# A Mamba-2 scan and its hardswish MLP on one core: the opening stage reordered

## The chip, the core and the metric

The kernel runs on one core of one Trainium2 chip. The core has five engines with an instruction list each: TensorE (PE in the profile; its weight loads are the row PEld), VectorE (DVE), ScalarE (ACT), GpSimd (POOL) and SyncE (SP, which here only issues transfers). They run beside each other and wait for one another by semaphores. Sixteen transfer engines (DMA) move data between the chip's memory and the core's. The metric is device microseconds of the one core, lower is better.

## The reference

The input `x` has 4 batches, 8 heads, 768 tokens and 32 channels; `B` and `C` have 16 states per head, `a` one decay per token. Per batch and head the scan is

```
cum   = cumsum(log(clip(a, 1e-6, 1)))                 # within a chunk
y     = ((C B^T) * exp(cum_i - cum_j) * (i >= j)) x   # within the chunk
      + (C state) * exp(cum_i)                        # from before it
state = exp(sum log a) * state + sum_j B_j x_j exp(cum_end - cum_j)
```

and its output, 3072 tokens of 256 channels, goes through an MLP: `h = y w_in` (256 to 2048), `g = h * clip(h + 3, 0, 6) / 6`, `out = g w_out` (2048 to 256). The MLP weights are 64-bit floats in memory.

## The kernel before

Tokens are worked in six chunks of 128 (times four batches: 512 columns). The order of every engine's list is written out by hand. Chunk 0 has a stage of its own: its scan, then its MLP in plain float32 products (`mlp_in` at L681, `first_out` at L801) while the weights are still being decoded. Chunks 1 to 5 use products of split operands (`squares`, `cross`, `wide_units`, `last_out`). The change touches the stage of chunk 0 and the first part of chunk 1's.

**Opening, to the first MLP product.** `a` comes in on SP's queue, then `C` (`pairs_first`, L99, eight transfers of 32 KB), `x` (L118) and weight piece 1 (`load_w`, L130). ACT's queue issues weight piece 0 and `B`. While `a` travels, PE writes the causal masks of chunks 0 and 1 into eight banks (`diff_mask`, L348), with thirty one-column products in between as filler. DVE scans the logs, `cum` (L288), and splits it into three bf16 parts, `split` (`in_three`, L293, last operation at L300). PE then adds to each bank the differences cum_i - cum_j: `diff_less` (L375) the subtrahend, `diff_pick` (L381) the minuend. For the first two batches of chunk 0 the minuend takes sixteen narrow products, one per head and half; for the other six (chunk, batch) pairs it takes two wide ones from rows that DVE first spreads over the heads (`spread_rows`, L277 to L281). ACT takes the exponentials (`diff_exp`, L400): four banks of chunk 0, later two of chunk 1, whose banks the state needs. `first_eto` (L402) and `turn_b` (L462) follow on PE and ACT. DVE transposes `C` (`turn_squares`, L500), masks it by parity (`part_heads`, L510) and applies `fade` (L516); PE multiplies the identity as filler (`busy`, L525). `scores` (L551) are 64 record pairs at L565 followed by the state's at L583; ACT copies the state (`take`, L599), DVE multiplies the scores with the decays (`multiply`, L614), PE forms the output in two halves (`mix`, L660, and `from_state`, L538), ACT copies it out (`keep`, L676), and `mlp_in` begins.

**Weights.** Each of eight pieces (four of `w_in`, four of `w_out`, 1 MB each as raw 64-bit words) is decoded to float32 by `decode` (L190): ACT copies the top 16 bits (L202), DVE takes the significand (L207, L211) and masks exponent and sign (L221, L223), ACT moves the exponent in two activations (L227, L229), DVE joins (L234) and multiplies (L244). It is a generator, and `weights(i, n)` advances it by n steps. There are three raw buffers; `load_w` for piece i + 3 waits for piece i to be read. A one-element `memset` into a buffer holds a transfer until DVE gets to it (L143, for piece 2 alone).

**First MLP.** `mlp_in(0, f)` for f = 0 to 15 uses four banks in turn, so f waits for the DVE operation at L798 (`times_ramp`) of f - 4, and every fourth f for the next piece of `w_in`. DVE decodes the pieces in between (`weave`, L1179). After it `first_out` runs in four passes of four batches; between them stand, among others, four PE transposes of `cum` (`turn_cum`, L334) with DVE's `by_token` (L338), which give the decays per token for chunks 2 to 5 (`cum_n`, first used by ACT at L420), the new state (`renew`, L631), the stores and loads of the decay rows on SP (`store_rows`, `load_eto`, `rows`), and the splitting of `w_in` (`in_parts`, L702).

## Time and profile before

| what | value |
|---|---|
| median of 3 runs | 337.93 us (337.47 to 337.95) |
| the profiled execution's own time | 337.99 us |
| its span | 336.2 us |
| PE busy | 329.7 us, 98% of the span |
| DVE busy | 265.4 us, 79% |
| ACT busy | 207.8 us, 62% |
| first MLP product of chunk 0 (L686) begins | 21.44 us |
| `first_out` of chunk 0 (L811) begins | 49.19 us |

Times inside an execution are microseconds from the span's start. The profile gives busy time per engine, the chain of work that ended last (each step followed back to what released it), groups of instructions by source line with what ended the idle time before them, and stretches of time with each engine's busy share. Matmuls are pipelined and their ends are modelled, so the distance from start to start is the better measure on PE. A float32 product shows as two records. "issue" is time in which an engine waited for nothing that the profile shows.

### The profile page before, as it was taken

The numbers are of one execution on the slowest core, as the hardware profiler recorded it, in microseconds if no ns is written. First come the engines' busy times: TensorE is split into PE (matmuls) and PEld (weight loads), VectorE is DVE, ScalarE is ACT, GpSimd is POOL, SyncE is SP. The second block draws the span as 40 slices with busy tenths as digits, with TensorE's granted clock in tenths as the row PEclk, the third lists the DMA queues.
The fourth block names the chain that finished last, engine by engine and source line by source line (L and its number), as shares of the span: only waits on it lengthen the run. The fifth ranks groups of instructions, "written<-read, shape, count | busy, mean of one in ns | idle before, by whom it ended". The sixth has DMA issues, their size and how long they took to land.

```text
span 336.2 us, 8325 instructions
## 1 busy us (share of the span) xinstructions
PE 329.7 (98%) x3361; PEld 272.4 (81%) x3361; DVE 265.4 (79%) x418; ACT 207.8 (62%) x448; POOL 130.3 (39%) x124
## 2 busy tenths in 40 slices
PE   7999999999999999999999999999999999999995
PEld 5464788888778888888888888888888888899994
DVE  6889999977899729969949558938678958599973
ACT  4788887747987571677662577643487221677661
POOL 2200000180744796179983078771058740000000
PEclk9999999999999999999999999999999999999999
DMA  8969960655950215229207258100142001210001
GB/s 174 168 251 225 197 253 19 171 75 140 178 39 1 61 34 116 47 35 108 49 2 162 36 73 76 37 4 10 27 71 20 2 4 17 29 20 0 2 0 62
DMA packets 89605, 25.15 MB, mean 75 GB/s; under 512 B 82208, under 2 KB 85952, under 8 KB 89056
## 3 DMA queue, kind: packets, MB, share of 16 engines
q1 hardware_dynamic: 85184, 23.33, 37.3%
q10 hardware_dynamic: 4384, 1.31, 1.8%
q8 instruction: 26, 0.43, 0.5%
q14 instruction: 11, 0.09, 0.1%
HBM read 21.33 MB, written 3.29 MB: 73 GB/s over the span
## 4 chain that ended last, share of the span: by engine, by line
PE 98%; POOL 0%; issue 0%; DVE 0%; ACT 0%; POOLq 0%
PE h L754 33%; PE wb L1002 9%; PE wc L1002 8%; PE o L811 8%; PE h L686 8%; PE wa L1002 8%; PE o_end L966 6%; PE wb L1010 3%; PE y L660 3%; PE y L538 2%; PE cb L565 2%; PE d L363 1%; PE y L583 1%; PE d L376 1%; PE d L528 1%; PE o_end L984 1%
## 5 line engine op out<-in xcount | busy, mean ns | idle before, releaser
L798 DVE SCALAR_TENSOR_TENSOR gT<-gT,h 128x512 f32<-128x512 f32 x96 | 64.6, 684 | 21.2 <-ACT gT L793 19.6
L793 ACT ACTIVATE gT<-h,half 128x512 f32<-128x512 f32 x96 | 65.4, 683 | 23.4 <-PE h L754 21.0
L774 ACT ACTIVATE h<-h 128x512 f32<-128x512 f32 x66 | 38.3, 585 | 36.6 <-PE h L754 36.5
L754 PE MATMUL h<-y_hi,w_part 128*128 128x512 f32 x160 | 51.1, 405 | 0.0
L754 PE MATMUL h<-y_less,w_part 128*128 128x512 f32 x160 | 50.1, 399 | 0.0
L754 PE MATMUL h<-y_lo,w_part 128*128 128x512 f32 x160 | 49.5, 395 | 0.0
L857 POOL TENSOR_TENSOR s<-gT 128x512 f32<-128x512 f32 x16 | 25.3, 1579 | 51.4 <-DVE gT L798 51.4
L754 PEld LDWEIGHTS h<-y_hi,w_part 128*128 128x128 f32 x160 | 29.9, 188 | 7.3 <-DVE gT L798 0.9
L754 PEld LDWEIGHTS h<-y_lo,w_part 128*128 128x128 f32 x160 | 30.0, 188 | 6.9
L420 ACT ACTIVATE L<-L,cum_n 128x64 f32<-128x64 f32 x128 | 31.7, 337 | 4.5 <-POOL L L162 4.5
L754 PEld LDWEIGHTS h<-y_less,w_part 128*128 128x128 f32 x160 | 29.1, 188 | 6.1 <-DVE h L771 0.3
L811 PE MATMUL o<-w_out,gT 128*128 128x256 f32 x128 | 29.1, 381 | 0.0
L686 PE MATMUL h<-yT,w_in 128*128 128x256 f32 (+1 forms) x96 | 27.8, 451 | 0.0
L438 POOL TENSOR_TENSOR tmp<-state,eto 128x256 f32<-128x256 f32 x5 | 3.4, 680 | 62.7 <-DVE state L593 56.0
L811 PEld LDWEIGHTS o<-w_out,gT 128*128 128x128 f32 x128 | 24.0, 190 | 3.4
L686 PEld LDWEIGHTS h<-yT,w_in 128*128 128x128 f32 x96 | 18.2, 190 | 9.3 <-issue 6.7
L857 POOL TENSOR_TENSOR gT<-gT 128x512 f32<-128x512 f32 x16 | 23.9, 1498 | 0.7
L894 DVE TENSOR_TENSOR q_part<-gT,q_part 128x256 fp32r<-128x256 f32 x24 | 21.5, 926 | 0.0
L431 POOL TENSOR_TENSOR bs<-B,L 128x128 f32<-128x128 f32 x24 | 12.0, 523 | 23.6 <-ACT L L420 15.7
L966 PE MATMUL o_end<-v_pair,g_pair 128*128 128x256 f32 x120 | 21.1, 281 | 0.0
L162 POOL TENSOR_SCALAR_AFFINE_SELECT L<-L 64x1024 f32<-64x1024 f32 (+1 forms) x16 | 20.0, 1255 | 2.0 <-DMA L<-cum_d 1.5
L857 POOL TENSOR_TENSOR s<-s,gT 128x512 f32<-128x512 f32 x16 | 20.5, 1290 | 0.0
(164 smaller groups left out, 636.0 us busy)
## 6 DMA issues: line engine op xcount, KB each, us to landing
raw<-in_moe_w_out_dram SPq DMA_DIRECT2D x4, 1024.0 KB
L<-cum_d SPq DMA_DIRECT2D x8, 512.0 KB
xt<-in_x_dram SPq DMA_DIRECT2D x6, 512.0 KB
raw<-in_moe_w_in_dram SPq DMA_DIRECT2D x3, 1024.0 KB
out_dram<-back SPq DMA_DIRECT2D x128, 16.0 KB
pairs<-in_C_dram SPq DMA_DIRECT2D x40, 32.0 KB
B<-in_B_dram SPq DMA_DIRECT2D x5, 256.0 KB
eto<-cum_e SPq DMA_DIRECT2D x20, 64.0 KB
```

What stands on the lines that cost most here:

```text
L162: nc.gpsimd.affine_select(out=t[rows], in_=t[rows], pattern=pattern, compare_op=ALU.is_ge, fill=-1e5, base=base, channel_multiplier=-1)
L420: nc.scalar.activation(Ls[c][:, b, h], Ls[c][:, b, h], AF.Exp, bias=cum_n[:, c, g:g + 1])
L686: nc.tensor.matmul(out=h[:, t:t + n], lhsT=w_in[f // FP][:, j, f % FP * P:(f % FP + 1) * P], rhs=yTs[k][:, j].rearrange("p b i -> p (b i)" ...
L754: nc.tensor.matmul(out=hs_[k, f], lhsT=w[j][:, f % FP * P:(f % FP + 1) * P], rhs=y[:, j], start=(start and j == 0), stop=True, skip_group_ ...
L774: nc.scalar.activation(h, h, AF.Copy, scale=1.0 / EPS + 1.0)
L793: nc.scalar.activation(gTs[k][:, f], h, AF.Relu, bias=half, scale=1.0 / 6.0)
L798: nc.vector.scalar_tensor_tensor(out=g, in0=g, scalar=1.0, in1=h, op0=ALU.min, op1=ALU.mult)
L811: nc.tensor.matmul(out=o[:, b % 2], lhsT=gTs[0][:, f, b * P:(b + 1) * P], rhs=w_out[:, f], start=(f == 0 and b % 2 == 0), stop=True, skip_ ...
L857: nc.gpsimd.tensor_tensor(out=o, in0=p_, in1=q_, op=op)
L894: nc.vector.tensor_tensor(out=l[:, j], in0=g[:, j], in1=h[:, j].bitcast(FP32), op=ALU.subtract)
L966: nc.tensor.matmul(out=ends_["cross" if n == 2 else "squares"][b], lhsT=g_parts[t][n][:, b * P:(b + 1) * P], rhs=w, start=(t == 0 and b < ...
L1002: nc.tensor.matmul(out=bank[:, slot], lhsT=lhs[:, j], rhs=rhs[:, j], start=(clear and j == 0), stop=True, skip_group_check=True)
```

## The change

- `C` of chunk 0 is loaded by head instead of by batch and head parity: still eight transfers of 32 KB, but the slowest dimension of each is now 32 groups of tokens rather than 4 heads.
- `x` of chunk 0 and weight piece 1 get a holding `memset`; `x` is issued after the first significand step of piece 0, piece 1 after `fade`.
- All (chunk, batch) pairs form their minuend by the sixteen narrow products; `spread_rows` and its two selectors go, and so do the thirty one-column products and `busy`.
- Piece 1 of the weights is decoded by a function of its own after `keep`, its exponents and results in two halves.
- In the first MLP, where a step of `weights` joins a piece (f = 4, 8, 12), it stands between `ramp` and `times_ramp`; the last sixteen products are no longer cut in two; the second significand step moves up one step.
- `renew(0)` moves from `first_out` to before `mix(0)`.
- `cum` by token comes from four small transfers, a DVE transpose and a POOL operation instead of PE transposes.
- The third piece of `w_in` is split earlier, and the buffers that `w_part` and `y_hi` take over change places.

```diff
@@ -100,2 +100,9 @@
             t = loads.tile([P, 2, NB, 4, N], FP32, name="pairs", tag="bc")
+            if c == 0:
+                for h in range(NH):
+                    rows = slice(h // 2 * 32, h // 2 * 32 + 32)
+                    nc.sync.dma_start(
+                        out=t[rows, h % 2].rearrange("s b a n -> s b (a n)"),
+                        in_=src[:, h, sl, :].rearrange("b (s a) n -> s b (a n)", a=4))
+                return t
             for b in range(NB):
@@ -120,2 +127,4 @@
         xts[c] = loads.tile([P, NB * NH, D], FP32, name="xt", bufs=1)
+        if c == 0:
+            nc.vector.memset(xts[c][:, 0, :1], 0)
         nc.sync.dma_start(out=xts[c], in_=x[:, :, sl, :].rearrange("b h s d -> s (b h) d"))
@@ -141,3 +150,3 @@
         raws[i] = raw
-        if i == 2:
+        if 0 < i < 3:
             nc.vector.memset(raw[:, :1], 0)
@@ -147,4 +156,2 @@
     load_bc(0)
-    load_x(0)
-    load_w(1)
     nc.scalar.preload_act_table_set("natural_log_exp_and_others")
@@ -189,2 +196,36 @@
 
+    def decode_halves(i):
+
+        n, cut = NK * FP * P, FP * P // 2
+        top = raws[i].bitcast(U16).rearrange("p (k f w) -> p k f w", k=NK, w=4)[..., 3]
+        lo, hi = (raws[i].rearrange("p (n w) -> p n w", w=2)[:, :, w] for w in range(2))
+        s = att.tile([P, n], U16, name="ws").rearrange("p (k f) -> p k f", k=NK)
+        e = att.tile([P, n], U16, name="we").rearrange("p (k f) -> p k f", k=NK)
+        m = att.tile([P, n], U32, name="wm")
+        halves = [slice(h * cut, (h + 1) * cut) for h in range(2)]
+        for h in halves:
+            nc.scalar.copy(out=s[:, :, h], in_=top[:, :, h])
+        nc.vector.tensor_scalar(
+            out=m, in0=hi, scalar1=0xFFFFF, scalar2=0x100000,
+            op0=ALU.bitwise_and, op1=ALU.bitwise_or)
+        for h in halves:
+            for t, mask in ((e, 0x7FF0), (s, 0x8000)):
+                nc.vector.tensor_scalar(
+                    out=t[:, :, h], in0=s[:, :, h], scalar1=mask, scalar2=None,
+                    op0=ALU.bitwise_and)
+            nc.scalar.activation(
+                e[:, :, h].bitcast(BF16), e[:, :, h], AF.Relu, bias=bias_hi, scale=-8.0)
+            nc.scalar.activation(
+                e[:, :, h], e[:, :, h].bitcast(BF16), AF.Relu, bias=bias_lo, scale=-1.0)
+        nc.vector.scalar_tensor_tensor(
+            out=m.bitcast(FP32), in0=lo, scalar=2.0 ** -32, in1=m, op0=ALU.mult, op1=ALU.add)
+        load_w(i + NRAW)
+        m = m.bitcast(FP32).rearrange("p (k f) -> p k f", k=NK)
+        for h in halves:
+            nc.vector.tensor_tensor(
+                out=e[:, :, h], in0=e[:, :, h], in1=s[:, :, h], op=ALU.bitwise_or)
+            nc.vector.scalar_tensor_tensor(
+                out=w_in[i][:, :, h], in0=m[:, :, h], scalar=2.0 ** -20,
+                in1=e[:, :, h].bitcast(BF16), op0=ALU.mult, op1=ALU.mult)
+
     def decode(i):
@@ -200,6 +241,3 @@
         m = att.tile([P, n], U32, name="wm")
-        for sl in (slice(0, n),) if i != 1 else (slice(0, n // 2), slice(n // 2, n)):
-            nc.scalar.copy(out=s[:, sl], in_=top[:, sl])
-            if i == 1 and sl.start == 0:
-                yield
+        nc.scalar.copy(out=s, in_=top)
 
@@ -218,2 +256,3 @@
             next(parts_m)
+            load_x(0)
             next(parts_m)
@@ -227,6 +266,6 @@
         nc.scalar.activation(e.bitcast(BF16), e, AF.Relu, bias=bias_hi, scale=-8.0)
+        next(parts_m, None)
         yield
         nc.scalar.activation(e, e.bitcast(BF16), AF.Relu, bias=bias_lo, scale=-1.0)
-        next(parts_m, None)
-        if i and i + NRAW < 2 * NP:
+        if i > 1 and i + NRAW < 2 * NP:
             load_w(i + NRAW)
@@ -254,5 +293,2 @@
     low = pre[:G, 10, :2 * P]
-    spread = [pre[:, 11 + c].bitcast(BF16).rearrange("k (h i) -> k h i", h=NH) for c in range(2)]
-    of_batch = const.tile([P, NB], BF16, name="of_batch")
-    of_head = const.tile([P, NH], BF16, name="of_head")
 
@@ -266,6 +302,2 @@
                 op=ALU.add)
-            nc.vector.tensor_reduce(
-                out=of_batch, in_=pick.rearrange("k (b h) -> k b h", b=NB), axis=AX.X, op=ALU.add)
-            nc.vector.tensor_reduce(
-                out=of_head, in_=pick.rearrange("k (b h) -> k h b", b=NB), axis=AX.X, op=ALU.add)
         nc.scalar.mul(less, pick, -1.0)
@@ -276,8 +308,2 @@
 
-    def spread_rows(c):
-
-        nc.vector.tensor_tensor(
-            out=spread[c], in0=split[:, c].unsqueeze(1).to_broadcast([P, NH, P]),
-            in1=of_head.unsqueeze(2).to_broadcast([P, NH, P]), op=ALU.mult)
-
     def log_a(sl):
@@ -333,9 +359,16 @@
 
-    def turn_cum(c_ps):
-        for c in range(2, NC):
-            nc.tensor.transpose(out=c_ps[:, c], in_=cum_c[:, c], identity=ident[:G, :G])
+    def spread_cum():
 
-    def by_token(c_ps):
-        nc.vector.tensor_scalar(
-            out=cum_n[:, 2:], in0=c_ps[:, 2:], scalar1=-1.0, scalar2=None, op0=ALU.mult)
+        cum_q = ffn.tile([P, NC - 2, G], FP32, name="cum_q", tag="wide")
+        for q in range(4):
+            nc.sync.dma_start(
+                out=cum_q[q * G:(q + 1) * G], in_=cum_c[:, 2:, q * G:(q + 1) * G])
+        return cum_q
+
+    def by_token(cum_q):
+        cum_t = ffn.tile([P, NC - 2, G], FP32, name="cum_t", tag="back")
+        nc.vector.transpose(
+            out=cum_t.rearrange("p c g -> p (c g)"), in_=cum_q.rearrange("p c t -> p (c t)"))
+        nc.gpsimd.tensor_scalar(
+            out=cum_n[:, 2:], in0=cum_t, scalar1=-1.0, scalar2=None, op0=ALU.mult)
 
@@ -355,7 +388,2 @@
             d = ps_y.tile([P, NH, HT], FP32, name="d", tag=f"y{b % 2}")
-        if (c, b) == (0, NB - 1):
-            for _ in range(30):
-                nc.tensor.matmul(
-                    out=d[:1, 0, :1], lhsT=ident_h[:, :1], rhs=hide[:, :1], start=True, stop=True,
-                    skip_group_check=True)
         n = NH // 4
@@ -381,9 +409,2 @@
     def diff_pick(c, b):
-        if c or b >= 2:
-            for a, rows in enumerate(HALF):
-                nc.tensor.matmul(
-                    out=ds[c, b][rows], lhsT=of_batch[:, b:b + 1].to_broadcast([P, HT]),
-                    rhs=spread[c][:, :, rows], start=False, stop=True,
-                    tile_position=(0, a * HT), skip_group_check=True)
-            return
         for h in range(NH):
@@ -524,9 +545,2 @@
 
-    def busy(n, bank):
-
-        for _ in range(n):
-            nc.tensor.matmul(
-                out=bank.rearrange("p (b i) -> p b i", b=NB), lhsT=ident,
-                rhs=ident.unsqueeze(1).to_broadcast([P, NB, P]), start=True, stop=True)
-
     def from_state(c, a, pairs=range(NQ)):
@@ -680,6 +694,6 @@
 
-    def mlp_in(k, f):
+    def mlp_in(k, f, between):
         h = ps.tile([P, TB], FP32, name="h", tag=f"f{f % 4}")
         for j in range(NK):
-            n = TB // (1 + (f * NK + j >= NF * NK - 16))
+            n = TB // (1 + (f * NK + j >= NF * NK - 0))
             for t in range(0, TB, n):
@@ -690,9 +704,5 @@
         ramp(k, f, h)
+        between()
         times_ramp(k, f, h)
 
-
-
-
-
-
     NJ = NF // 2
@@ -718,3 +728,3 @@
 
-        hi = one(const, f"w{i - 1}" if i > 1 else f"hi{i}")
+        hi = one(const, {2: "w0", 3: "w2"}.get(i, f"hi{i}"))
         lo = one(const, f"lo{i}") if i < 2 else one(att, "wm") if i == 2 else two("ws")
@@ -734,3 +744,3 @@
     def split_y(k):
-        hi = const.tile([P, NK, TB], F32R, name="y_hi", tag="w0")
+        hi = const.tile([P, NK, TB], F32R, name="y_hi", tag="w1")
         lo = att.tile([P, NK, TB], F32R, name="y_lo", bufs=1)
@@ -886,3 +896,3 @@
         hi, lo, less = quarter_parts[k] = [], [], []
-        homes = ((ffn, "wide"), (ffn, "back")), ((const, "w0"), (att, "y_lo"))
+        homes = ((ffn, "wide"), (ffn, "back")), ((const, "w1"), (att, "y_lo"))
         for where, g in zip(homes, halves):
@@ -1106,5 +1116,6 @@
 
-    def results(c):
+    def results(c, more=None):
         if c == 1:
             keep(c)
+            next(more)
         split_y(c)
@@ -1142,7 +1153,5 @@
         mask_again(0, b)
-    for c in range(2):
-        spread_rows(c)
+    weights(0, 1)
     diff(0, 0, 1)
     diff(0, 2, 3)
-    weights(0, 1)
     for b in range(NB):
@@ -1150,8 +1159,7 @@
     first_eto()
-    diff(1, 2, 3)
     weights(0, 1)
+    turn_b(0)
+    diff(1, 2, 3)
     for b in range(NB):
         ends(0, b)
-    turn_b(0)
-    diff(1, 0, 1)
     weights(0, 2)
@@ -1159,2 +1167,3 @@
     diff_exp(1, 3)
+    diff(1, 0, 1)
     turn_squares(bcs[0][0], turned(0)[2])
@@ -1162,14 +1171,13 @@
     fade(0, HALF[1])
+    load_w(1)
     weights(0, 1)
-    busy(2, ps.tile([P, NB * P], FP32, name="d", tag="f3"))
     scores(0)
     multiply(0)
+    weights(0, 1)
     load_w(2)
     load_w(3)
-    weights(0, 1)
-    weights(1, 1)
+    renew(0)
     mix(0)
-    keep(0, lambda: weights(1, 1))
-    weights(1, 3)
-    weights(1, 1)
+    keep(0)
+    decode_halves(1)
     load_bc(1)
@@ -1188,5 +1196,7 @@
             for f in range(NF):
-                mlp_in(k, f)
+                late = [i for i in weave.get(f, []) if f == 4 * i - 4]
+                mlp_in(k, f, lambda: [weights(i, 1) for i in late])
                 for i in weave.get(f, []):
-                    weights(i, 1)
+                    if i not in late:
+                        weights(i, 1)
                 if f in (6, 8):
@@ -1195,2 +1205,3 @@
             add_up(ends_at[1])
+            cum_q = spread_cum()
             store_rows()
@@ -1209,8 +1220,4 @@
                         next(ins[n])
-                    if (i, b) == (1, 0):
-                        renew(0)
                     if (i, b) == (1, 1):
-                        c_ps = ps.tile([P, NC, G], FP32, name="c_ps", tag="f1")
-                        turn_cum(c_ps)
-                        by_token(c_ps)
+                        by_token(cum_q)
                     if (i, b) == (2, 0):
@@ -1227,3 +1234,3 @@
                         load_bc(ahead)
-                        for n in (0, 0, 1):
+                        for n in (0, 0, 1, 2):
                             next(ins[n])
@@ -1239,4 +1246,3 @@
                         own_products(c)
-                        results(c)
-                        next(ins[2])
+                        results(c, ins[2])
                         decay(ahead, 2)
@@ -1251,3 +1257,2 @@
             next(ins[2])
-            next(ins[2])
             continue
```

More of the change, by code (lines that the diff above doesn't have):

```diff
@@ L1162 @@
     fade(0, HALF[1])
+    load_w(1)
     weights(0, 1)
-    busy(2, ps.tile([P, NB * P], FP32, name="d", tag="f3"))
     scores(0)
     multiply(0)
+    weights(0, 1)
     load_w(2)
     load_w(3)
-    weights(0, 1)
-    weights(1, 1)
+    renew(0)
     mix(0)
-    keep(0, lambda: weights(1, 1))
-    weights(1, 3)
-    weights(1, 1)
+    keep(0)
+    decode_halves(1)
     load_bc(1)
```

## The prediction

> **What bounds the kernel now.** I read the page first (PE busy 98% of the span, and 98% of the chain that ended last), then the chain in order of time, then ACT, DVE and the transfers of the first 22 us. From 21.44 us on the chain is PE without a break worth 0.1 us, so a saving counts only if it starts PE's first MLP product earlier or takes work from PE's own list. The chain of waits, columns start, length, what:

> ```profile
> 6.63 1.28 PE d L371 x3
> 7.92 0.85 PE d L376 x2
> 8.77 0.99 PE d L392 x17
> 9.76 0.60 PE d L376 x2
> ...
> 17.65 0.38 ACT adds L599
> ...
> 19.62 0.26 PE y L660 x12
> 19.88 0.20 issue
> 20.08 0.75 PE y L660 x44
> 20.83 0.61 PE y L538 x16
> 21.44 27.74 PE h L686 x96
> ...
> 59.55 0.36 PE c_ps L336 x4
> ```

> See three things: two L376 products take 0.85 us at 7.92 but 0.43 from 11.14 on, so PE runs at half rate until about 9.9 us; a wait for ACT's `adds` stands in the middle; and PE waits 0.20 us for nothing but its next instruction. Then ACT and DVE in order of time:

> ```profile
> 9.38 1.08 ACT L400 ACTIVATE L<-d 128x512 f32<-128x512 f32 x2 [1.40 <-PE d L392]
> 10.74 1.08 ACT L400 ACTIVATE L<-d 128x512 f32<-128x512 f32 x2 [0.28 <-PE d L384]
> 12.75 0.59 ACT L466 COPY bT<-t_ps 128x512 f32<-128x512 f32 x1 [0.64 <-PE t_ps L457]
> 15.47 1.06 ACT L400 ACTIVATE L<-d 128x512 f32<-128x512 f32 x2
> 7.42 2.36 DVE L279 TENSOR_TENSOR pre<-split,of_head 128x1024 bf16<-128x1024 bf16 x2
> 13.02 1.12 DVE L500 STREAM_TRANSPOSE csT<-pairs 128x512 f32<-128x512 f32 x1 [0.27 <-DMA pairs<-in_C_dram]
> ```

> ACT goes almost without a gap from 9.38 to 16.53. The last pair of exponentials frees the banks into which L583 adds the state; L583 begins at 16.75 and feeds `adds`, which feeds L660. So ACT's list, not C or DVE, is what ends last before the MLP. The last view is the stretches of the transfers (the last two columns are the share of the 16 transfer engines and GB/s):

> ```profile
> 8.00:9.00 1.00, 1.00 (x14) 0.30 (x14) 1.00 (x2) 0.00 (x0) 0.00 (x0) 1.00 0.40 44
> 18.00:19.00 1.00, 0.93 (x66) 0.84 (x67) 1.00 (x3) 1.00 (x4) 0.00 (x0) 1.00 0.01 4
> ```

> From 8 to 11 us only some 0.4 of the engines work, on C and the tail of B; at 18 us all is loaded.

> **The change part by part.**

> *Spread rows and fillers out, head products in.* DVE loses L279 (2.36 us) and two reductions (0.39 us). PE loses 30 one-column products (0.82 us in the chain), the four L528 (1.91 us), and six pairs of wide picks; it gains 6 x 16 narrow ones. Sixteen narrow ones took half of 0.99, 0.50 us, at half rate, the four wide of two batches 0.55, 0.28 each: +0.22 x 6 = 1.3 us of PE before the scores, less at full rate. Without the fillers L371 ends near 6.9, so the first L376 starts when its weights follow `split` (DVE L300 ends 7.39), at 7.55 instead of 7.71. PE then goes: batch 0, 1 to 9.4; L376 to 10.1; first half of the next batch 10.4; all 10.9; `e_ps` and `t_ps` to 11.8; the four of chunk 1 (2 x 0.43 and 2 x 0.5, with the 0.1 gaps of the trace) to 13.3-13.5. Scores can start then, against 15.54.

> *DVE.* After 7.39: L207 0.73, memset 0.06, L211 1.14, L221 0.45, L223 0.46, L500 1.12, L510 0.88: `cT` at 12.3, if C has landed by 10.3. C now spreads over 16 engines instead of some 0.4 of them, so it and B should be in by about 10; if not, the cost is that of today's landing (12.9), which puts `cT` at 15.0, still before today's 15.1.

> *ACT, the deciding list.* First pair of exponentials 9.22-10.30 (-0.16); third starts when its product has drained, 10.7 (no spread to wait for, and `t_ps` now stands ahead of chunk 1, so the 0.64 wait goes); fourth ends 11.75, `eto` 12.1, `bT` 12.64, L227 and L229 (1.18 and 1.06 start to start) 14.88, chunk 1's pair 15.95 instead of 16.53: 0.58 us. L583 follows at 16.2, `adds` at 17.1, and L660 begins 0.58 earlier, at 17.5. DVE covers this: L234 waits for L229 and ends 15.65, two L614 end 16.9. From L660 to the MLP the trace has 3.3 us, of which the wait at 19.88, with its emptied pipe, is 0.2 to 0.4. MLP start 20.4 to 20.8; I take 20.6, so **-0.77 us**.

> *x and weights held.* x goes out behind DVE's L207 (8.2, not 9.61) and has 4 us of packets, so it lands near 13.5; L583 needs it at 16.2. Piece 1 goes out behind the `fade` (12.8, not 10.31 behind x) and takes some 4.5 us: 17.5, needed when `keep` ends at 21. Cost nothing, with 3 us to spare. Pieces 2 and 3 go out as now (19.2, 19.4).

> *Piece 1 in halves, `renew` forward.* `renew` (0.45 + 0.6 us of DVE) now stands before piece 1's decoding; that is hidden by `keep`. ACT does two copies and four activations of half size after `keep` (bounded by 0.34 us, half of a whole 0.68, and 0.68 each; near the upper end, as a 512-wide copy took 0.68 with its latency): first half of w_in[1] at 24.9, second 25.8; product f=4 needs it at 20.6 + 4 x 1.73 = 27.5. In the rest of the first MLP DVE is full. Going through its list with L221/L223/L207 1.35 us, L211 1.14, L234 + L244 1.83 and L798 0.62, the tightest places are w_in[2], 33.2 against 34.4, and the bank of f=8, which waits for f=4's L798, now behind L234 and L244: 33.85 against 34.4. The cover is 0.55 us; beyond it each us of DVE is a us of PE.

> *`cum_n` without PE.* Four transposes go: **-0.36 us**. In their place four small transfers on SP, one DVE transpose (a quarter of L500's 1.12, 0.28, what L339 took) and one POOL operation (at most L431's 0.69). SP's stores and `eto` loads move back by four issues of up to 0.62 us, 2.5 us: `eto` may land at 64, half a us after ACT wants it; ACT then has 4.55 us of idle time before L420 at 71.88. POOL's operation stands ahead of `tmp`, `bs` and `conceal`, late by at most 0.7 us, which L420 and chunk 2 (scores at 112) absorb.

> *Rest.* The last 16 MLP products in one piece: 64 records of 0.2159 against 32 of 0.4293, **-0.08 us**. Other homes of w_part and y_hi: ins[2]'s two copies move into ACT's idle 4.55 us; `y_lo` on DVE starts 0.3 us later, with L754 on y_lo over 1 us behind. Nothing.

> Sum -0.77 - 0.36 - 0.08 = -1.2 on the profiled execution's 337.99 (span 336.2 and 1.8 around it; the median of the runs is 337.93): **336.8 us**. Ends of the unknown terms: the MLP start gains nothing (instruction wait, below) to 1.75 us (full rate at 6.5 us: ACT's list starts 0.6 earlier and runs to 15.0, scores at 12.4).

> [...] L376's 0.85 and 0.43 us show the clock at half until 9.9 us, with PE busy since 2.13. [...]

> **The rivals.**

> 1. *PE's instructions come late.* The 0.20 us stall is at PE's 705th record. In the queue of instructions a packet of 16 KB starts at 10.1, 17.9 and 24.0 us, each about 1.1 us after PE passed records 154 and 410 where nothing stood before it; the one for 705 ended at 18.8 and PE went on 1.26 us later. The third stayed out while piece 2 was moved (20.4 to 23.9). In the new order record 410 lies 48 records into the scores, at 13.9, so its packet is due at 15.0, and piece 1's packets run from 13.8 to 17.2. If it waits for them, PE has its instructions at 17.2 + 0.95 + 1.26 = 19.4, needs them at 18.1, and the MLP starts 2.5 us after, 21.9: 337.99 + 0.5 - 0.44 = 338.0, no change. For it: the third packet. Against: when the clock is early the scores start at 12.4 and the packet is level with piece 1. [...]

> [...]

> 3. *DVE becomes the bound in the first MLP (slower).* The bank of f=8 has 0.55 us of cover. `renew`, the extra instructions of the halves and the later turn of f=4's L798 all lie before it. From 0.55 us late PE waits; from 2.4 us late the whole gain is gone and more: at 2.6 us late 338.7. For it: DVE is full from 24 to 55 us. Against: it starts 1.3 us earlier than now, after L614, and the sum above has its durations.

> **How the numbers follow.** Forecast 0.58, rival 1 0.18, rival 2 0.06, rival 3 0.18. About 0.2% (0.7 us) is what a measurement of this kernel tells from no change: below 337.25 faster, above 338.6 slower. Forecast alone: 335.6 to 337.25; with rivals 1 and 2 and the near part of 3, 335.6 to 338.4. Faster 0.59 (the forecast), same 0.23 (rivals 1, 2), slower 0.18.

> **What would show it.** First L686 near 20.6 in the chain; ACT's chunk-1 pair ending near 16.0; L500 without a wait for C; no c_ps; 27.5 us of L686 without a gap. A wait "issue" over 1 us in L660 shows rival 1, two L376 of 0.85 us after 10.5 rival 2, PE idle on DVE L798 or w_in between 27 and 48 us rival 3. A wait of L583 for x, or of the copies for piece 1, would make the working of the held loads wrong.

## The result: slower by 1%, and where the time went

The changed kernel takes 344.38 us (median of four executions, 339.27 to 346.10) against 337.88 (337.47 to 337.95); the ratio is 1.011, with an interval of 1.007 to 1.014. Of the four, 345.15 and 346.10 us lie over 1.5% above the fastest and are left out of the ratio; the fastest, 339.27 us, is the only one with a full mean clock (0.999, the others 0.988 to 0.990). The profiled execution took 343.62 us, its span is 341.9, 5.7 more than before. From its page, the span, PE's busy time and the granted clock in 40 slices:

```profile
span 341.9 us, 8362 instructions
PE 328.8 (96%) x3375; PEld 267.4 (78%) x3375; DVE 261.6 (76%) x420; ACT 208.7 (61%) x450; POOL 130.1 (38%) x125
PEclk9969999999999999999999999999999999999999
```

PE is busy for 0.9 us less than before, so what was added is waiting, and the third slice (17 to 26 us) has a clock of 0.6. The chain in order of time (start, length, what) says where the waiting is:

```profile
16.70 0.68 PE y L674 x41
17.38 2.00 issue
19.38 0.63 PE y L674 x19
...
23.21 29.20 PE h L700 x64
52.41 13.81 PE o L821 x64
66.22 0.87 PE t_ps L478 x8
...
179.54 0.91 issue
...
227.47 0.84 issue
...
279.72 0.86 issue
```

Read it against the chain of before, whose steps were `mix` (L660 there, L674 here) at 18.07, first MLP product at 21.44, `first_out` at 49.19 and the turn of the next `B` and `C` (t_ps) at 63.55:

| stretch | before | after | change |
|---|---|---|---|
| up to `mix` | 18.07 | 16.70 | -1.37 |
| `mix` to first MLP product | 3.37 | 6.51 | +3.14: the wait 2.00 instead of 0.20, and 1.34 of half rate |
| first MLP | 27.74 | 29.20 | +1.46 |
| `first_out` with the `cum` transposes, to t_ps | 14.36 | 13.81 | -0.55 |
| three waits "issue" in later chunks | 0 | 2.61 | +2.61 |
| rest of the span, not traced | | | +0.4 |

The chain has one more long "issue", 1.19 us at 166.50. It stands on VectorE's part of the chain; TensorE has no gap there.

The opening did become 1.37 us shorter. A wait of 2.00 us "issue" inside `mix` takes that back, a fall of the clock takes another 2.8, and three more waits of the same kind, at 180, 227 and 280 us among products that the change does not touch, take 2.6. The stretches of time of the same execution show PE's busy time (the second number) and the clock (the third from the end):

```profile
18.00:19.00 1.00, 0.00 (x0) 0.00 (x0) 1.00 (x1) 0.00 (x0) 0.00 (x0) 1.00 0.89 352
20.00:22.00 2.00, 2.00 (x81) 1.81 (x80) 0.79 (x2) 0.74 (x2) 0.00 (x0) 0.50 0.84 227
26.00:28.00 2.00, 2.00 (x6) 0.96 (x5) 1.93 (x5) 1.97 (x5) 0.00 (x0) 0.94 0.48 81
```

PE does nothing from 18 to 19 us while the transfer engines run at 352 GB/s, and from 20 us on it is busy all the time at half the clock. The trace's record of the clock has it at half from 19.43 to 26.26 us, at full from 5.78 to 19.43.

What the transfer engines moved is weight piece 1, from 15.68 to some 20.2 us. The queues of the transfers, first from 15.5 to 17.1 us, then from 17.1 to 18.3 us (packets, MB, share of the engines):

```profile
q1 hardware_dynamic: 76, 0.31, 88.4%
...
q1 hardware_dynamic: 106, 0.43, 89.3%
q8 instruction: 1, 0.02, 5.0%
```

The one instruction packet (16 KB) starts at 17.18, ends at 18.14, and PE goes on at 19.38. PE had passed record 410, from which the prediction's rival 1 counts the request, at 14.52, so the packet started 2.65 us after it. In the kernel before it started 1.08 us after it (16.80 and 17.88).

### The profile page after: what moved, and what is told of

Its sections match the earlier page's. It is cut to its first block, busy times and chain, and to the rows that moved or that the text cites. A ratio compares the mean times of both kernels' runs of the same rounds, so it can differ in the third digit from the quotient of the medians.

```text
span 341.9 us, 8362 instructions
## 1 busy us (share of the span) xinstructions
PE 328.8 (96%) x3375; PEld 267.4 (78%) x3375; DVE 261.6 (76%) x420; ACT 208.7 (61%) x450; POOL 130.1 (38%) x125
## 4 chain that ended last, share of the span: by engine, by line
PE 91%; DMA 3%; DVE 2%; issue 2%; ACT 0%; SPq 0%; DVEq 0%
PE h L764 33%; PE h L700 9%; PE wc L1012 8%; PE o L821 8%; PE wb L1012 8%; PE wa L1012 8%; PE o_end L976 6%; PE wb L1020 3%; PE y L674 3%; PE y L552 2%; DMA raw<-in_moe_w_in_dram 2%; PE cb L579 2%; DMA pairs<-in_C_dram 1%; PE y L597 1%; DVE q_part L904 1%
## 5 line engine op out<-in xcount | busy, mean ns | idle before, releaser
L808 DVE SCALAR_TENSOR_TENSOR gT<-gT,h 128x512 f32<-128x512 f32 x96 | 64.7, 683 | 23.5 <-ACT gT L803 21.9
L700 PE MATMUL h<-yT,w_in 128*128 128x512 f32 x64 | 29.3, 620 | 0.0
L700 PEld LDWEIGHTS h<-yT,w_in 128*128 128x128 f32 x64 | 12.7, 201 | 15.8 <-issue 14.5
L867 POOL TENSOR_TENSOR gT<-gT 128x512 f32<-128x512 f32 x16 | 23.9, 1503 | 0.7
L867 POOL TENSOR_TENSOR s<-s,gT 128x512 f32<-128x512 f32 x16 | 20.5, 1291 | 0.0
L452 POOL TENSOR_TENSOR bs<-B,L 128x128 f32<-128x128 f32 x24 | 11.0, 480 | 23.5 <-ACT L L441 15.8
```

The costliest lines, as they stand in the source:

```text
L700: nc.tensor.matmul(out=h[:, t:t + n], lhsT=w_in[f // FP][:, j, f % FP * P:(f % FP + 1) * P], rhs=yTs[k][:, j].rearrange("p b i -> p (b i)" ...
L808: nc.vector.scalar_tensor_tensor(out=g, in0=g, scalar=1.0, in1=h, op0=ALU.min, op1=ALU.mult)
L867: nc.gpsimd.tensor_tensor(out=o, in0=p_, in1=q_, op=op)
```

## The experiments

On the four chips used, the kernel before had medians of 337.63, 337.89, 338.02 and 337.70 us, in the order of the groups of runs below; each ratio is against the runs on the same chip.

TensorE's records (weight loads, products and some thirty semaphore steps alike) are counted here from the start of the trace. Before has 6754, after 6779. The wait in `mix` stands at record 705, the later three at 4033, 5057 and 6081: all of these differ by multiples of 256, and the page of either kernel has 26 packets of 16 KB in the instruction queue, one per 256 records. That gave the theory, the author's reading of these two traces: instructions come in blocks of 256 records; crossing the edge of one asks for the next but one, which PE needs 256 records after the edge, or 295 after what it executes at that moment (of the 26 packets of either trace none starts more than 0.01 us ahead of the record 39 before its edge); with some 1.1 us to the packet's start (1.08 behind record 410, before), 0.95 us for it (0.94 and 0.96 at 17.88 and 17.18 us) and 1.2 to 1.5 us until PE goes on (1.24 to 1.54 at the four waits of the changed kernel), 295 records that are done in under some 3.3 us, an estimate from these sums, end in a wait, and so does a packet that finds piece 1's packets ahead of it (2.65 us to its start). Ahead of the three late waits the 295 records took 2.3, 2.2 and 3.0 us; ahead of the same records in the kernel before they took 4.3, 3.6 and 4.8. The rivals: the fillers that were removed had kept the clock up; holding `x` and piece 1 was the only fault; or DVE is late.

### Only the record count, only the hold

`e1_align` writes seven of the eight masks in two products instead of four, 28 records fewer:

```diff
-        n = NH // 4
+        n = NH // 4 if (c, b) == (0, 0) else NH // 2
```

> The changed kernel with 28 PE records fewer in its opening (the causal masks of seven banks are written by two products of 256 columns instead of four of 128, the same PE time). The theory: PE gets its instructions in blocks of 256 records, the block edges of the changed kernel lie 28 records deeper in the work than before, and that is why PE stands still for 0.91, 0.84 and 0.86 us at its records 4033, 5057 and 6081. With the edges back in their old places these three waits go (0.04 us in all in the kernel before), 2.6 us less than the changed kernel, 336.7 us where the clock stays full and 341 us where it falls to half; the wait of 2.0 us in the first mix stays. The rival, that late data or transfers of the chunks cause the three waits: they stay, and the time is that of the changed kernel.

Measured: 341.73 us, ratio 1.012 (1.010 to 1.014). The three late waits are gone. The opening is worse: the packet for record 449 starts at 13.41 us (11.85 in the changed kernel), and PE, in the middle of the scores, has to wait for it. Why it starts later was not tried. Its chain has waits of 1.10 us there and 1.85 at 705, the clock is at half for 10.24 us, and the MLP starts at 24.40.

`e2_hold` moves `load_w(1)` of the changed kernel one DVE operation later, behind `weights(0, 1)`:

> The changed kernel with weight piece 1 held for one DVE operation more (0.7 us), so that it is issued behind the joining of piece 0's exponents. The theory: PE's block of instructions, asked for at 14.5 us and due at 15.6, meets piece 1's packets, whose first starts at 15.7; with piece 1 at 16.4 the block is in by 16.6 and usable by 17.9, PE waits 0.5 instead of 2.0 us, and without the long wait PE's clock stays full, so the first MLP product starts near 20.4 (23.2 now) and its 64 records take 27.6 us (29.2 now). The three later waits stay. Time 337.8 us in every run. The first rival, that the fillers taken out let the clock fall: the wait shrinks but half rate comes in most runs all the same, 341 us or more. The second rival, that the block's delay has nothing to do with piece 1: the wait of 2.0 us stays.

Measured: 343.55 us, ratio 1.015 (1.010 to 1.019). The packet for 705 now starts at 15.64, ahead of piece 1 (16.23), and the wait falls from 2.00 to 1.05 us. It doesn't vanish, and the clock still falls, for 6.83 us.

`e3_both` has both edits:

> Both edits together. The theory: 337.8 less 2.6, 335.2 us, below the kernel before, with no half rate after 6 us. With either rival the time stays above 338 us.

Measured: 343.40 us, ratio 1.017 (1.015 to 1.019), no late waits, but 1.09 us at record 449 and 3.00 at 705, whose packet starts at 19.44, again near the end of piece 1 (16.16 to 19.82). The clock stays at full behind the first of these waits and is at half for 6.83 us behind the second.

`e4_before_hold` is the kernel before with piece 1 held until after `fade`, and nothing else:

```diff
-        if i == 2:
+        if 0 < i < 3:
             nc.vector.memset(raw[:, :1], 0)
...
-    load_w(1)
...
     fade(0, HALF[1])
+    load_w(1)
```

> The kernel before with one part of the change alone: piece 1 held for DVE until after the fade, 5 us later than now; all fillers and wide products stay. The theory: PE asks for its block at 16.8 us, piece 1's packets then start at 16.7 and delay it, so PE waits 2 us or more in the first mix instead of 0.2, and the clock may fall to half after it although both fillers are there: 340 us, up to 344 where it falls. The rival, that the fillers keep the clock: the wait alone, at most 340 us in every run. If the held load does no harm: 338 us.

Measured: 341.74 us, ratio 1.012 (1.011 to 1.014). Its chain:

```profile
19.75 2.45 issue
...
23.80 29.13 PE h L685 x96
```

The same place in the work, 2.45 us instead of before's 0.20; the packet started at 19.92, 3.25 us after record 410 and near the end of piece 1 (its packets start from 16.58 to 20.33). The clock then fell for 3.41 us, with both fillers in place. So the hold alone, the step which the prediction had put at nothing, costs 4.1 us (341.74 against 337.63 on the same chip).

### The fillers as a cause, and the record count as a dose

`g4_more` is the kernel before with sixty one-column products instead of thirty (60 records more); `g3_nofill` is the kernel before without them and without `busy` (68 fewer), and with all 32 last MLP products cut, so that later edges stay within four records of where they were:

```diff
-            for _ in range(30):
+            for _ in range(60):    # g4_more; range(0) in g3_nofill
```

> The kernel before with sixty instead of thirty one-column products: 60 records more, 0.8 us of TensorE in the opening while it waits for the cumulated sums in part. Nothing is left out of the result. Theory (record edges): 60 records move the edges of every later stage into stretches that use 256 records in 2.2 us; stalls called issue of about 1.1, 1.6, 1.6 and 1.5 us near 80, 176, 223 and 273 us, none of them in the kernel before, and perhaps a longer one in the opening: 342 to 345. Rival (the number of records is harmless, only the 0.8 us of work counts): at most 338.8, no issue line over 0.3 us after 20 us.

> The kernel before without its thirty one-column products and its two busy products, 68 records fewer, and with all 32 (not 16) of the last MLP products cut in two, 64 records more, so that the records of all later stages stay within 4 of the kernel before. Nothing is left out of the result. Theory (only the place of the record edges and the packets matter): no late stalls, the stall at record 705 falls 8 to 17 products later in the work and stays under 0.5 us, granted clock full after 10 us: 336.9 to 337.6. Rival (the fillers keep the clock up): half rate for at least 3.4 us after 13 us without a stall of over 1 us ahead of it, 339 or more.

`g4_more` took 346.72 to 356.51 us, median 348.20, ratio 1.029 (1.026 to 1.032). Four late waits stand where the theory had put them, 1.4 to 1.5 us each in the chain, against 1.1 to 1.6 forecast:

```profile
18.67 1.22 issue
...
82.28 1.39 issue
...
180.24 1.50 issue
...
228.80 1.46 issue
...
280.83 1.39 issue
```

Thirty products more, 0.8 us of work, cost 8.8 us in the shortest of the four executions: the record count is a cause by itself. The opening is also worse than forecast: 1.22 us at record 705, and half rate for 3.41 us.

`g3_nofill` took 346.75 us, ratio 1.027 (1.024 to 1.029), against a forecast of 336.9 to 337.6. It has no late wait, as forecast, but the opening failed. PE in order of time (the bracket: idle time ahead, and what ended it):

```profile
15.02 1.83 PE L565 MATMUL cb<-cT,bT 32*64 32x128 f32 x64 [2.56 <-DVE cT L510]
...
20.11 0.31 PE L583 MATMUL y<-xt,bs 64*32 64x64 f32 x1 [2.16 <-issue]
```

The stretch from 16 to 17 us of the same execution (the clock is the third number from the end):

```profile
16.00:17.00 1.00, 1.00 (x50) 0.67 (x42) 0.08 (x2) 0.00 (x0) 0.00 (x0) 0.50 0.96 389
```

The clock is at half already at 16 us, ahead of the first instruction wait: PE had stood 2.56 us for DVE's `cT`, where `busy` used to fill the time. That is the rival's mechanism, and in the order of before it holds. The second fault is a new place of the edge: the scores begin at record 194, one behind an edge (193). PE crosses it only when `cT` releases it, so the packet for 449 is asked for at 15 us, comes at 17.67 behind piece 1, and two waits of 2.16 and 2.68 us follow.

### Putting the opening right

`g1_wide` is the changed kernel with the wide minuends back, piece 1 issued behind `x` without the later hold, and 31 of the last MLP products cut (18 records fewer than before in all); `g2_wide_hold` is the same with piece 1 held as in the change.

```diff
+        if c or b >= 2:    # the wide products of before
...
+    for c in range(2):
+        spread_rows(c)
...
+            load_w(1)      # g1_wide, behind load_x(0)
```

> The changed kernel with three parts undone: the wide products from spread rows are back, the last 31 products of the first MLP are cut in two again, and piece 1 goes out behind x as before. The fillers stay out; all else stays changed. Theory (TensorE's instructions come in blocks of 256 records, each asked for some 39 records ahead of the edge; a stretch that uses 256 records in under about 3.3 us stalls, and so does a block that waits behind piece 1's packets): records in the later stages are 19 fewer than in the kernel before, where no stall was seen; the block for record 705 comes before piece 1. Stall at 705 at most 0.4 us, granted clock full from about 6 us to the end, first MLP product at 20.5 to 20.9, none of the three late stalls of 0.8 to 0.9 us: 336.0 to 336.6. Rival (the removed fillers let the clock fall): half rate for 3.4 to 6.8 us after 17 us with no stall ahead of it, 339 to 342. Rival (VectorE has become the bound of the first MLP): gaps in L700, first_out no earlier than 49.2 even where the MLP starts earlier.

> As the run with the wide products back and the MLP's products cut, but with piece 1 held behind fade as in the change. Theory (instruction block behind piece 1): the block is asked for at about 16 us, when piece 1's packets are being moved until about 20; stall of 1 to 2.5 us at record 705, half rate for 3.4 to 7 us after it, no late stalls: 338.5 to 341.5. If holding piece 1 costs nothing, as the prediction had it: the same time as that run within 0.4 us.

`g1_wide` missed: its executions took 345.68, 345.86 and 346.48 us, and one 336.76 at a mean clock of 0.999, so there is no ratio; the same list of instructions can run either way. In the profiled one (346.48) the scores again begin at record 194, as in `g3_nofill`: waits of 3.43 and 2.96 us at 449 and 705, half rate for 13.65 us, no late wait. `g2_wide_hold` took 341.11 us, ratio 1.009 (1.006 to 1.012): waits of 1.30 and 0.62 us, half rate for 6.83 us. The comparison of the two says nothing on the hold, since both have an edge in the worst place.

`h1_aligned` and `h2_chunk1` put the edge elsewhere. Both issue `x` and piece 1 straight behind `C`. `h1_aligned` has `g1_wide`'s wide products and twenty one-column products (scores at record 234, 22 records fewer than before in all); `h2_chunk1` has the wide products for chunk 1 alone and no filler (scores at 250, also 22 fewer):

```diff
-        if c or b >= 2:
+        if c:              # h2_chunk1
...
+            for _ in range(20):    # h1_aligned: one-column products
```

> The run with the wide products back, with two things more: x and piece 1 are issued straight behind C, without a hold, and twenty one-column products stand before the last mask again, so that the scores begin 40 records later in the instruction blocks (record 234 instead of 194, 40 behind an edge instead of one); 20 instead of 31 of the last MLP products are cut, which leaves the records of the later stages 22 short of the kernel before. Theory (blocks of 256 records, asked for when the edge before is crossed, and a packet that waits behind piece 1): the block of the scores is there in time, piece 1 is through by about 17, the stall at record 705 is 0.3 to 0.7 us, the clock stays full from 6 us on, scores at 14.5, first MLP product at 20.4 to 20.9, no late stalls: 335.8 to 336.6. Rival (holding off the clock's fall takes the old fillers and busy): half rate after 17 us without a stall of 1 us, 339 or more. Rival (x in front disturbs C): scores no earlier than 15.3, 337.3 to 337.7.

> The changed kernel with the wide products back for chunk 1 alone (all four batches of chunk 0 keep the narrow ones, no filler), x and piece 1 issued straight behind C without a hold, the last 16 MLP products cut as before. The scores begin at record 249, 56 behind an edge. Theory (blocks and packets): as the run with twenty fillers, stall at record 705 of 0.3 to 0.7 us, full clock, no late stalls; VectorE has one spread less, TensorE 56 narrow records more: 335.8 to 336.6. Rival (without any filler the clock falls): half rate after 17 us, 339 or more.

The profiled executions took 337.13 and 336.93 us, with the clock at full from 7.9 and 7.4 us to the end and no late waits. From the chain of `h2_chunk1`:

```profile
15.63 0.43 issue
...
18.84 0.77 issue
...
20.93 27.74 PE h L719 x96
...
62.48 0.87 PE t_ps L497 x8
...
95.67 1.63 DVE w_part L755
...
98.02 0.61 DVE gT L827
...
111.93 1.11 PE cb L598 x60
```

The MLP starts 0.5 us earlier than before, its 27.74 us are those of before to the digit, and the clock needs no filler here: PE waits 0.56 us for `cT`, in `h1_aligned` 1.39 us, where `g3_nofill` had 2.56. But over ten executions the medians are 337.85 and 337.62 us against 338.02, ratios 1.002 (0.999 to 1.006) and 1.000 (0.997 to 1.002): three of the ten of each took 339.4 to 345.2 us at a mean clock of 0.98 to 0.99. Only one execution of each was profiled, with waits of 0.4 to 0.8 us at the edges; whether longer ones stand behind the longer times isn't shown.

`i4_unheld` is the changed kernel with nothing undone but the two holds:

> The changed kernel with one thing undone: x and piece 1 of the weights are issued straight behind C, without a hold. Records unchanged. Theory (two causes in the opening: the packet behind piece 1, and the place of the block edge): piece 1's packets run from 13 to 17.5 us, the block for record 705 is asked for at about 15 us and must still wait for them until 17.3, so the stall stays at 1.5 to 2.2 us, half rate follows, and the three late stalls of 0.8 to 1.2 us stay: 342 to 344.5. Rival (the hold was the only fault of the opening): stall at 705 under 0.7 us, clock full, MLP start at 20.5 to 20.9, time 338.2 to 339.5 with the late stalls.

Measured: 344.44 us, ratio 1.016 (1.010 to 1.022). The sum came as forecast; the shape did not. The packet for 449 now starts at 13.4 us (11.85 in the changed kernel), and there are two opening waits, 1.21 us at 449 and 0.80 at 705; half rate for 10.24 us; the three late waits are there (0.87, 1.02, 0.32 in the chain). Hold and record count are both causes, and undoing the hold alone gains nothing in this order.

### Two single parts, and what is late next

`h3_cum` is the kernel before with `cum` by token from transfers, DVE and POOL; `h4_c` is the kernel before with `C` loaded by head.

> The kernel before with one part of the change: cum by token from four small transfers, a VectorE transpose and a GpSimd operation in place of TensorE's four transposes; renew stays where it was. The prediction's term for it is -0.36 us. Theory (blocks): eight records fewer leave the later edges in the harmless stretch, so the term stands: 337.4 to 337.7. If the SP transfers disturb the decay rows, a wait of ACT's L420 group for eto after 70 us and no gain: 337.9 or more.

> The kernel before with one part of the change: C of chunk 0 by head over all transfer engines; x and piece 1 behind it as before, records unchanged. If C set the end of the opening, cT would be ready 1 us earlier and the MLP too: 337.0. Theory (ACT's list sets it, as the prediction read the chain): C lands 0.5 to 1.5 us earlier, scores start up to 1 us earlier, but L583 and its adds still wait for ACT's last pair of exponentials, so that L660 moves by at most 0.3 us and the stall at record 705 grows by as much: 337.6 to 338.1.

`h4_c`: 338.00 us, ratio 1.000 (0.998 to 1.001). The scores start at 15.10 instead of 15.54, the wait at 705 grows to 0.73 us, the MLP starts at 21.54. `C` isn't what moved them: in `h3_cum` and `i3_before_later`, whose opening is that of the kernel before, the scores start at 15.03 and 15.13 and the wait is 0.75 and 0.57 us, with the clock at full from 7.85 and 8.11 us instead of 9.87. As forecast, an earlier `C` alone is worth nothing.

`h3_cum`: 338.18 us, ratio 1.000 (0.999 to 1.001), against a forecast gain of 0.36. Its chain reaches t_ps at 62.95 instead of 63.55, and then two waits stand in chunk 1; PE in order of time:

```profile
90.48 0.72 PE L761 MATMUL h<-y_hi,w_part 128*128 128x512 f32 x2 [0.16 <-DVE gT L805]
...
96.88 0.73 PE L761 MATMUL h<-y_hi,w_part 128*128 128x512 f32 x2 [0.59 <-DVE gT L805]
```

Chunk 2's scores begin at 112.92, against 112.70 before. The other outcome that was named, ACT late for want of `eto`, didn't come: that group waits for POOL's `L`, as in the kernel before. In `h2_chunk1` the same wait shows as `w_part` and `gT` on DVE in the chain above: 1.07 us ahead at t_ps, 0.77 ahead at chunk 2's scores. There DVE, which splits the fourth piece of `w_in` between the `gT`, is busy for 14.9 of the 15 us from 92 to 107.

To see whether the order of these steps is to blame, `i1_cum_later` (on `h3_cum`), `i2_chunk1_later` (on `h2_chunk1`) and the control `i3_before_later` (on before) move them back:

```diff
-                if f in (4, 5, 7):
+                if f in (4, 5, 9):
                     next(ins[3])
-                if f in (9, 11, 13):
+                if f in (11, 13, 14):
                     next(more)
```

> The run with cum by token without TensorE, and in chunk 1 the last step of the split of w_in's fourth piece two MLP rows later (9 instead of 7) and the first three sums of w_out at rows 11, 13 and 14 instead of 9, 11 and 13. Theory (VectorE's list between 90 and 105 us takes the gain of the removed transposes): TensorE's waits of 0.16 and 0.59 us for gT near 90 and 97 us shrink to 0.3 us together or less, chunk 2 starts 0.4 to 0.7 us earlier: 337.3 to 337.6. Rival (the lists were not the cause, or the steps are only late elsewhere): 337.9 to 338.6, with a wait of similar size at another place before 125 us.

> The run with the wide products for chunk 1 alone and unheld loads, with the same shift of VectorE's steps in chunk 1. Theory: the 0.9 us that TensorE lost near 98 us is regained for the most part, 336.1 to 336.6 where the clock stays full. Rival (only late elsewhere): 336.8 or more.

> The kernel before with nothing but the same shift of VectorE's steps in chunk 1, as the control. TensorE had only 0.03 us of idle time in this stretch, so by the theory (the lists are late only where TensorE comes earlier) nothing moves: 337.7 to 338.1. If the shift itself helps or hurts, this run shows by how much.

`i1_cum_later`: 338.37 us, ratio 1.002 (1.001 to 1.003). Chunk 2's scores begin at 112.67, and the wait has gone to a later place; PE in order of time:

```profile
111.97 0.70 PE L1009 MATMUL wb<-gT,t 128*128 128x256 f32 x2 [0.31 <-DVE gT L805]
```

`i2_chunk1_later`: 337.12 us, ratio 0.999 (0.997 to 1.002); its profiled execution has the same new wait near 111 us. `i3_before_later`: 338.40 us, ratio 1.003 (1.002 to 1.004), so the shift by itself loses a little. The rival held: moved in this way the steps are only late elsewhere. DVE's list up to chunk 2's scores is full, and a gain made earlier is partly lost there. No kernel here beats the one before by more than the measurement can tell.

## Why the prediction was wrong, by its own steps

**The term that failed: the MLP start, forecast 0.77 us earlier, measured 1.77 us later (23.21 against 21.44).** The sum carried an earlier L660 through to the MLP and put the held loads at nothing. Both steps were wrong, as the next three points show. (From 21.44 to the 20.6 taken is 0.84, not 0.77; nothing rests on the difference.)

**The opening up to `mix`: right in direction, larger than forecast.** Forecast was 0.58 us at L660, measured 1.37. The clock was at full from 5.78 us, not 9.9, near the upper end that the prediction named (full rate at 6.5). No run shows the ground for that 6.5; it was the author's assumption, and what the runs show in its place is a spread. In part it goes with the missing one-column products: full rate begins at 5.06 to 7.94 us in the ten profiles without them and at 7.85 to 9.87 in the six with thirty. In part it is luck: `e2_hold` and `i4_unheld`, with the changed kernel's list on PE, have 5.43 and 7.94. `C` was read as landing by 10; it landed at 11.88, and DVE's L500 (here L521) waited for it, as DVE's list in order of time has it:

```profile
12.06 1.10 DVE L521 STREAM_TRANSPOSE csT<-pairs 128x512 f32<-128x512 f32 x1 [1.73 <-DMA pairs<-in_C_dram]
```

SP's eight issues of `C` last from 1.25 to 8.4 us, and the chain has the last transfer from 7.98 to 11.88; the working had weighed the transfer engines and not the issues. `cT` at 14.09 was inside the cover named (15.0). But the chain up to `mix` now runs through `C`, `cT` and the scores, which end at 15.4, and not through ACT's list, whose last pair ended at 15.3.

**"L660 begins 0.58 earlier ... MLP start 20.4 to 20.8": an earlier `mix` didn't carry through.** `h3_cum`, `i1_cum_later` and `i3_before_later` have the opening of the kernel before, and with an earlier clock they begin L660 at 17.48 to 17.63 instead of 18.07. Their first MLP product begins at 21.32 to 21.43, at most 0.12 us earlier, for the wait at record 705 has grown from 0.20 to between 0.57 and 0.75 us. From the chain of `i3_before_later`:

```profile
19.38 0.57 issue
...
21.32 27.74 PE h L686 x96
```

The instruction packet starts between 17.57 and 17.90 us in all four, while piece 1 is still being moved (until 18.1 to 18.3). The prediction read the wait at 19.88 as 0.2 to 0.4 us that could be saved. It is the next bound, and it takes most of what is gained in front of it.

**"x and weights held ... Cost nothing, with 3 us to spare": the step that failed.** Piece 1 came at some 20.2 us, not 17.5, and its first reader, DVE's L208, waited 0.70 us for it; that cost nothing, since DVE then stood 2.71 us for ACT's copies. What cost time is that its packets stood in front of PE's instructions (from 15.68 us, the instruction packet at 17.18). `e4_before_hold` prices it alone at 4.1 us on the kernel before. The working asked only who reads piece 1, not who else uses the transfer engines while it is under way. In the changed order the hold isn't the only fault: `i4_unheld` undoes it and gains nothing, since the packet for 449 is late there.

**Rival 1 was the case, with a chance too low and a price too small.** It had PE needing record 705 at 18.1 and having it at 19.4; measured are 17.38 and 19.38. The argument against it, that an early clock would bring the packet level with piece 1, did not hold: the clock was early, but the scores started at 14.23, not 12.4, behind the late `C`, and piece 1's packets began at 15.68, ahead of the packet at 17.18. Its price, 338.0, lacked three things: the clock fell behind this wait (first MLP product at 23.21, not 21.9; L700 29.20 us, not 27.66), and the later waits. From 338.0: +1.3 for the start, +1.5 for L700, -0.2 since the transposes were worth 0.55, +2.6 for the three late waits, +0.4 rest: 343.6, the profiled time.

**"Sixteen narrow ones ...: +0.22 x 6", "thirty one-column products out", "in one piece": counted in time, not in records.** Together with `busy` and the transposes they move later work by 25 records. That costs 2.6 us near 180, 227 and 280 us, which no step of the prediction mentions. `e1_align` takes the 28 records back and the waits go; `g4_more` adds 60 to the kernel before and gets four. In every run of this study the late waits are there at 25 and 60 more, and absent from 22 fewer to one more.

**`cum_n` without PE: -0.36.** On PE's list it was worth more, 0.55 us up to t_ps. `h3_cum` shows it gone again by chunk 2's scores. The prediction asked whether `eto` and POOL would be late, not whether DVE could follow PE in chunk 1.

**Rival 3, DVE in the first MLP: not seen.** `h2_chunk1` starts its MLP 0.5 us earlier and needs the same 27.74 us; the cover of 0.55 us sufficed there. DVE became the bound one stage later. **Rival 2, two L376 of 0.85 us after 10.5: not seen.** No run shows a ground for its chance of 0.06; the clock was at full from 5.78 to 19.43 us. The split products' -0.08 us lies under the half rate and was not measured alone.

Three things stay open. How long a wait may be before the clock falls isn't settled: 2.45 us was enough in `e4_before_hold`, 1.10 in `e1_align` and 1.05 in `e2_hold`, while 1.09 us in `e3_both` was not, and the profiled `h2_chunk1` with 0.43 and 0.77 stayed at full though some of its other executions have a lower mean clock. In one of four executions each, the changed kernel, `e2_hold` and `i4_unheld` had a full mean clock (339.27, 340.67 and 340.50 us). Why the packet for 449 starts late in `i4_unheld` was not tried apart. And no run has the whole change without these waits, so what it would be worth then isn't measured.

## What to carry to other kernels

Where one engine is busy for 98% of the span, ask of every edit how many instructions it adds or takes from that engine's list and which stretch the block edges then fall on, not only how long the work is: here 25 records more cost 2.6 us, far behind the change. A transfer that nobody waits for can still cost time: piece 1, held, put the instruction packet at 19.92 us instead of 17.88 and cost 4.1 us (`e4_before_hold`), so look at what is on the transfer engines when a fast stretch needs its next block. And before counting a gain, follow it to the next engine that is full: a microsecond won on PE by 62 us was partly gone by 112.
